# The first chunk's normalization on ScalarE and VectorE, its turns a block ahead, and two loads moved, in an attention and GLU kernel on one Trainium2 core

## The chip, the cores and the metric

The kernel runs on one core of a Trainium2 chip. The time is device microseconds of one execution. Six runs of the kernel before are shown by their median; one more execution was profiled.

The engines are written as the profile writes them: PE is TensorE (matmuls; PEld its weight loads), DVE is VectorE, ACT is ScalarE, POOL is GpSimd, and SP is SyncE, which here issues DMAs. SPq and ACTq are the queues through which SP and ACT issue DMAs.

## The reference

x has 2048 tokens of 512 values, all in bf16. One normalization of x feeds both parts.

```python
xn = (x - mean(x)) / sqrt(var(x) + 1e-5)

# A: attention, 32 heads of 16, each token sees the 256 tokens up to itself
q, k, v = split(xn @ wqkv)                      # wqkv 512 x 1536
p = softmax(where(0 <= i - j < 256, q @ k.T / 4, -1e9))
a = (p @ v) @ wo                                # wo 512 x 512

# B: gated bilinear, F = 1792
b = ((xn @ w_gate) * (xn @ w_up)) @ w_down

out = x + a + b
```

## The kernel before

The 2048 tokens are worked in four chunks T = 0..3 of 512 tokens, each of four blocks b of 128 tokens. For each chunk there are 14 gate groups `gT.f` and 14 up groups `uT.f` (four matmuls of 128x512 each, a "dense group"), projections to queries, keys and values, scores and weighted values of the attention, and the sums `downT.b` of 14 matmuls with `Wd` and four with `Wo`, which end in one PSUM bank and are added to x and stored. The sums of the last chunk are cut into two `Sums`: `down3.b` and `wo3.b`.

The program order is made when the kernel is built. The class `Kernel` holds a planner: `list_work` lists the work, and `loop` (line 309) plays it through with costs and due times written in the code (for example `PSUM_COPY`, and `land`, `wv`, `wk`, `wq` in `first_chunk`), emitting instructions in the order it arrives at. On the chip each engine runs its instructions in that order and waits for semaphores. What the planner knows are:

- `Op`: a step on DVE (`V`), ACT (`A`), POOL (`G`) or SP (`S`), with the engines that may take it and their costs. Copies out of PSUM may go to DVE or ACT.
- the list `A` of `Dense` groups for PE, of which the planner looks at the first `WINDOW` = 4, and the list `B` of `Sums`, of which only the first is looked at.
- scores: 76 batches S0 to S75, each eight to twenty small matmuls into one PSUM tile `S`, then an exponential on ACT (`P<-S`, line 476) of up to 2048 columns; no batch can start before the exponential of the one before has read `S`. `PACE` = 3.0 is the least distance between batches in the plan. Parts of P are then masked, either by selects on POOL (`i_select`, line 209) or by ANDs on DVE (`i_and`, line 215).
- values: V0 to V15, one after the batches of a (chunk, head group) pair, followed on DVE by two transposes, a reciprocal, a product and a transpose back.

Four PSUM banks `M0` to `M3` hold what PE writes for all but the scores; a bank is free again when a copy on DVE or ACT has read it.

`prologue` issues the loads. `x` of block 0, then `Wqkv` in three parts (values at 1024, keys at 512, queries at 0), then gate and up weights in halves, the rest of `x`, `Wd` and `Wo` go through SP's queue; `x` of blocks 1 to 3 goes through ACT's. POOL makes the identity matrix `ident`, and PE then runs 40 warm-up matmuls on it (line 180). ACT runs one exponential on a single column (line 170), which brings its function table in.

`first_chunk` is about chunk 0, the part most changed. Per block: `i_stats` (lines 241 to 243: statistics, mean and variance `mv`, and `ve` = variance + 1e-5) on DVE, `i_root` (line 247: `rs` = `ve` to the power -0.5) on POOL, `i_apply` (line 252: `xn` = (x - mean) * rs) on DVE, `turn` (line 576: four transposes of `xn` on PE), a copy to `xnT`, and then on PE the values `v0.b` (line 634), keys `k0b{b}` and queries `q0b{b}` (16 matmuls of 128x128 each). They are added to the list `A` block by block:

```python
self.add(f"turn{b}", 1.1, [ap], turn, turned)
self.add_v(0, b, wv)
self.add(f"k0b{b}", 4.2, [("xnT", 0, b), wk], lambda i, f=project: f(i, 512), k_out)
self.add(f"q0b{b}", 4.2, [("xnT", 0, b), wq], lambda i, f=project: f(i, 0), q_out)
```

With the window of four, PE's order comes out as turn0, v0, k0, turn1, q0, turn2, k1, q1, k2, q2, turn3, v1, v2, v3, k3, q3, g0.0, u0.0, S0 (v0 for `v0.0`, k0 for `k0b0` and so on). Blocks of later chunks are normalized by `norms` in the shadow of other work and transposed by DMA.

Of the kernel before, what the change touches and what calls it, by code (L numbers as in the profile page):

```python
# [8 lines left out]
F32 = mybir.dt.float32  # L9
# [76 lines left out]
class Kernel:  # L86
    PBUFS = 7
    WINDOW = 4
    PACE = 3.0
    SHARE = 1.0  # L90

    def __init__(self, live=True):
        self.live = live
# [4 lines left out]
    def open(self, ctx, tc, x, wqkv, wo, wg, wu, wd, out):  # L98
        self.tc, self.nc = tc, tc.nc
        self.x_d, self.out_d = x.flatten_outer_dims(), out.flatten_outer_dims()  # L100
        self.w_d = dict(qkv=wqkv, o=wo, g=wg, u=wu, d=wd)
        self.F = wg.shape[1]

        def pool(name, bufs, **kw):
            return ctx.enter_context(tc.tile_pool(name=name, bufs=bufs, **kw))

        c = self.const = pool("const", 1)
        self.work, self.few = pool("work", 3), pool("few", 2)
        psum = pool("psum", 1, space=bass.MemoryType.PSUM)

        def some(name, n, shape, dtype=BF16):
            return [c.tile(shape, dtype, name=f"{name}{i}") for i in range(n)]

        self.x = c.tile([128, NT, 512], BF16, name="x")
        self.Wqkv = c.tile([128, 4, 1536], BF16, name="Wqkv")
        self.Wo = c.tile([128, 4, 512], BF16, name="Wo")
        self.Wg = c.tile([128, 4, self.F], BF16, name="Wg")
        self.Wu = c.tile([128, 4, self.F], BF16, name="Wu")
        self.Wd = c.tile([128, NF, 512], BF16, name="Wd")
        self.Q = some("Q", 2, [128, 4, 512])  # L120
        self.K = some("K", 3, [128, 4, 8, 2, 64])
        self.V = some("V", 3, [128, 8, 16, 18])
        self.xnT = some("xnT", 2, [128, 4, 512])
        self.hT = some("hT", 2, [128, NF, 512])
        self.OT = some("OT", 2, [128, 4, 512])
        self.P = some("P", self.PBUFS, [128, 4, 512])
        self.xn = some("xn", 4, [128, 512])
        self.mv = some("mv", 2, [128, 4, 2], F32)
        self.rs = some("rs", 2, [128, 4], F32)
        self.ve = c.tile([128, NT], F32, name="ve")  # L130
        self.at = c.tile([128, 16, 2, 32], F32, name="at")
        self.on = c.tile([128, 16, 2, 16], BF16, name="on")
        self.ident = c.tile([128, 128], BF16, name="ident")
        self.own = c.tile([128, 2], F32, name="own")
        self.mhalf = c.tile([128, 4], F32, name="mhalf")
        self.masks = c.tile([128, 5, 64], I16, name="masks")
        self.S = psum.tile([128, 4, 512], F32, name="S")
        self.M = [psum.tile([128, 512], F32, name=f"M{i}") for i in range(4)] + [self.S[:, 3, :]]

    def prologue(self):  # L140
# [4 lines left out]
        def load(eng, dst, src):  # L145
            eng.dma_start(out=dst, in_=src)

        load(nc.sync, self.x[:, 0, :], xv[:, 0, :])
        for t in range(1, 4):
            load(nc.scalar, self.x[:, t, :], xv[:, t, :])  # L150
        for lo in (1024, 512, 0):
            load(nc.sync, self.Wqkv[:, :, lo:lo + 512], w["qkv"][:, :, lo:lo + 512])
        h = self.F // 2
        for lo in (0, h):
            load(nc.sync, self.Wg[:, :, lo:lo + h], w["g"][:, :, lo:lo + h])
# [1 line left out]
            if lo == 0:  # L157
                load(nc.sync, self.x[:, 4:8, :], xv[:, 4:8, :])
        load(nc.sync, self.x[:, 8:NT, :], xv[:, 8:NT, :])
        load(nc.sync, self.Wd[:], w["d"])  # L160
        load(nc.sync, self.Wo[:], w["o"])

        c = self.const
# [3 lines left out]
        nc.gpsimd.memset(self.mhalf[:], -0.5)  # L167
        warm = c.tile([128, 1], F32, name="warm")
        nc.vector.memset(warm[:], 0.0)
        nc.scalar.activation(out=warm[:], in_=warm[:], func=ACT.Exp)  # L170
        pi = c.tile([128, 1], I32, name="pi")
        nc.gpsimd.iota(pi[:], pattern=[[0, 1]], base=0, channel_multiplier=1)
        podd = c.tile([128, 1], I32, name="podd")
# [166 lines left out]
    def choose(self):  # L340
# [25 lines left out]
        for n, d in enumerate(self.A[:self.WINDOW]):  # L366
            t = self.when(d.deps)
            if t is not None and free:
                t = max(t, free[0][0], now)
                t += SWITCH * (d.mode != self.mode) + SWITCH * (d.mode == "C" and self.mode == "D")  # L370
                if a is None or t < a[0]:
                    a = (t, n)
        if self.B:
            d = self.B[0]
            t = self.when(d.deps)
            if t is not None and ("bank" in d.link or free):
                b = max(t, now if "bank" in d.link else max(now, free[0][0]))
# [148 lines left out]
    def list_work(self):  # L526
        self.first_chunk()
        for T in range(NCH):
            if T + 1 < NCH:
                self.norms(T + 1)  # L530
            for f in range(NF):
                self.add_gate(T, f)
            if T + 1 < NCH:
                self.add_qk(T + 1, 0)
                for b in range(4):
                    self.add_v(T + 1, b)
                for c in range(1, 4):
                    self.add_qk(T + 1, c)
        for T in range(NCH):
            for b in range(4):  # L540
                self.add_down(T, b)

    def add(self, *a):
        self.A.append(Dense(*a))
# [6 lines left out]

    def first_chunk(self):

        land = (3.7, 3.7, 4.6, 5.2)
        wv, wk, wq = 6.3, 7.8, 9.3
        st = [self.op(f"st{b}", {"V": (0.96, 1.05)}, [land[b]], lambda e, b=b: self.i_stats(b, self.mv[0]), rank=3 + b)
              for b in range(4)]
        roots = []
        for lo, hi in ((0, 1), (1, 2), (2, 4)):
            r = self.op(f"rs{lo}", {"G": (0.6 if hi - lo == 1 else 0.73, 0.62 if hi - lo == 1 else 0.75)}, st[lo:hi],  # L560
                        lambda e, lo=lo, hi=hi: self.i_root(0, lo, hi - lo), rank=0)
            roots += [r] * (hi - lo)
        last = self.op("masks", {"G": (0.33, 0.4)}, [r], lambda e: self.nc.gpsimd.memset(self.masks[:], -1), rank=9)
        for n in range(5):
            last = self.op("masks", {"G": (0.4, 0.5)}, [last], lambda e, n=n: self.i_masks(n), rank=9)
        self.at_["masks",] = last
# [2 lines left out]
                self.V[n][:, :, :, 16:18], 1.0), rank=9)  # L569
        for b in range(4):  # L570
            tok = slice(128 * b, 128 * b + 128)
            ap = self.op(f"ap{b}", {"V": (0.38, 0.48)}, [roots[b]], lambda e, b=b: self.i_apply(b), rank=0)

            def turn(i, b=b):
                for k in range(4):
# [26 lines left out]
                for c in range(4):  # L602
                    self.at_["Q", 0, c, b] = x

            self.add(f"turn{b}", 1.1, [ap], turn, turned)
            self.add_v(0, b, wv)
            self.add(f"k0b{b}", 4.2, [("xnT", 0, b), wk], lambda i, f=project: f(i, 512), k_out)
            self.add(f"q0b{b}", 4.2, [("xnT", 0, b), wq], lambda i, f=project: f(i, 0), q_out)
# [85 lines left out]
    def add_down(self, T, b):  # L694
        h = [("up", T, f) for f in range(NF)]
        o = [("OT", T, c) for c in range(4)]
        if T < NCH - 1:
            emit, evac = self.sum_of(T, b, slice(0, 512))
            self.B.append(Sums(f"down{T}.{b}", T, b, 0, 18, h + o, 2, emit, evac, {}))
            return  # L700
        late = [] if b < 2 else [("attended", T)]
        halves = [(slice(0, 512), {}, MM)]
        if b == 3:
            halves = [(slice(0, 256), {}, MM / 2), (slice(256, 512), {"bank": 4}, MM / 2)]
            late += [("S", len(self.batches) - 1)]
        for n, (cols, link, mm) in enumerate(halves):
            emit, evac = self.sum_of(T, b, cols)
            name = f"{T}.{b}{'ab'[n]}"
            self.B.insert(len(self.B) - b - n, Sums("down" + name, T, b, 0, NF, h + late, 7, emit, lambda o, i: None, link, mm))
            self.B.append(Sums("wo" + name, T, b, NF, 18, o, 4, emit, evac, link, mm))  # L710

    def sum_of(self, T, b, cols):
        tok, t, keep = slice(128 * b, 128 * b + 128), 4 * T + b, {}
# [60 lines left out]
```

## Time and profile before

| | |
|---|---|
| median of six runs | 269.22 us (268.84 to 269.45) |
| profiled execution | 268.92 us |
| its span | 266.9 us |
| PE busy | 260.7 us, 98% |
| DVE busy | 189.5 us, 71% |
| ACT busy | 163.6 us, 61% |
| POOL busy | 123.0 us, 46% |
| DMA in the second of 40 slices (6.67 us each) | 376 GB/s |

How to read the profile: a timeline line gives the start in us from the span's start, the time it took, engine, line of the kernel, operation, what it writes and reads, shapes, and the count of instructions merged into it; in square brackets stands how long the engine was idle before it and what released it. A line of waits gives who waited, for whom, the total in us, how often, and the longest. The chain of work that ended last is followed back from the last instruction, at each step to what released it; its lines give start, duration and what it was. PE's matmuls are pipelined and the shown durations overlap, so the distances between starts tell more than the durations.

### The profile page before, as it was taken

How to read it: one execution, taken by the hardware profiler on the slowest of the kernel's cores; microseconds unless marked ns; L12 is line 12 of the kernel's file. 1: busy time of each engine (PE TensorE's matmuls, PEld its weight loads, DVE VectorE, ACT ScalarE, POOL GpSimd, SP SyncE). 2: the span in 40 equal slices, each digit the busy share in tenths (PEclk: the TensorE clock that was granted, in tenths of full speed). 3: DMA queues.
4: the chain of work that ended last, by engine and by line, in shares of the span. 5: the costliest groups of instructions: out<-in, count | busy, mean ns of one | idle time of the engine just before them, and what ended most of it. 6: DMA issues, size and time to landing. Idle time of an engine off the chain costs nothing.

```text
span 266.9 us, 7983 instructions
## 1 busy us (share of the span) xinstructions
PE 260.7 (98%) x3450; PEld 131.1 (49%) x3450; DVE 189.5 (71%) x361; ACT 163.6 (61%) x118; POOL 123.0 (46%) x276
## 2 busy tenths in 40 slices
PE   7999999999999999999999999999999999999994
PEld 6884344654544444464443444356443444353562
DVE  5879978879995717788997716878882628778224
ACT  2315666877786566768677567667786567657100
POOL 3501675646357180735539180825537180825500
PEclk9999999999999999999999999999999999999999
DMA  6999630000003010000002210000000000000002
GB/s 229 376 375 348 172 42 2 4 0 2 4 13 69 22 41 25 0 2 2 0 2 48 57 39 22 0 4 2 2 2 20 22 23 22 0 2 0 2 2 79
DMA packets 17186, 13.87 MB, mean 52 GB/s; under 512 B 7040, under 2 KB 17152, under 8 KB 17152
## 3 DMA queue, kind: packets, MB, share of 16 engines
q1 hardware_dynamic: 16576, 12.91, 15.9%
q8 instruction: 27, 0.44, 0.7%
q10 hardware_dynamic: 576, 0.46, 0.5%
q14 instruction: 7, 0.06, 0.1%
HBM read 9.70 MB, written 2.10 MB: 44 GB/s over the span
## 4 chain that ended last, share of the span: by engine, by line
PE 95%; DVE 1%; DMA 1%; ACT 1%; issue 0%
PE M L192 72%; PE S L200 9%; PE M L224 7%; PE M L634 6%; DMA x<-in_A_x_dram 1%; ACT P L476 1%; PE S L192 1%; DVE st L241 0%; PE M L576 0%; DVE xn L724 0%; ACT xnT L186 0%; DVE mv L242 0%; DVE xn L252 0%; DVE ve L243 0%
## 5 line engine op out<-in xcount | busy, mean ns | idle before, releaser
L476 ACT ACTIVATE P<-S 128x2048 bf16<-128x2048 f32 x76 | 140.9, 1853 | 57.0 <-PE S L200 54.3
L209 POOL TENSOR_SCALAR_AFFINE_SELECT P<-P 64x256 bf16<-64x256 bf16 (+1 forms) x248 | 113.7, 460 | 116.9 <-ACT P L476 104.0
L192 PE MATMUL M<-xnT,Wg 128*128 128x512 bf16 x224 | 57.7, 380 | 0.0
L192 PE MATMUL M<-xnT,Wu 128*128 128x512 bf16 x224 | 57.7, 380 | 0.0
L192 PE MATMUL M<-Wd,hT 128*128 128x512 bf16 (+1 forms) x224 | 51.5, 373 | 0.0
L685 DVE TENSOR_TENSOR hT<-M,gsb 128x512 bf16<-128x512 f32 x56 | 38.0, 679 | 9.2 <-PE M L192 8.9
L192 PEld LDWEIGHTS <-hT 128*128 128x128 bf16 x238 | 21.6, 98 | 24.2 <-issue 3.2
L192 PEld LDWEIGHTS <-Wu 128*128 128x128 bf16 x224 | 20.4, 98 | 25.3 <-issue 2.8
L512 DVE STREAM_TRANSPOSE at<-M 128x512 f32<-128x512 f32 x32 | 22.3, 707 | 14.6 <-PE M L224 14.6
L192 PEld LDWEIGHTS <-Wg 128*128 128x128 bf16 x224 | 19.9, 98 | 24.9 <-issue 4.1
L192 PE MATMUL M<-xnT,Wqkv 128*128 128x128 bf16 (+1 forms) x224 | 30.6, 288 | 0.0
L200 PE MATMUL S<-Q,K 32*128 32x320 bf16 (+3 forms) x720 | 30.0, 254 | 0.1
L188 DVE CAST gsb<-M 128x512 bf16<-128x512 f32 x36 | 24.7, 686 | 5.4 <-PE M L192 5.2
L200 PEld LDWEIGHTS <-K 32*128 32x128 bf16 x720 | 12.0, 92 | 32.1 <-issue 31.1
L215 DVE TENSOR_TENSOR P<-P,masks 128x512 int16<-128x512 int16 x56 | 23.0, 418 | 6.2 <-ACT P L476 6.2
L724 DVE TENSOR_TENSOR y<-M,x 128x512 bf16<-128x512 f32 x12 | 8.3, 688 | 20.5 <-PE M L192 20.3
L263 DVE TENSOR_SCALAR K<-M,own 128x512 bf16<-128x512 f32 x27 | 19.2, 745 | 4.6 <-PE M L192 4.6
L192 PEld LDWEIGHTS <-Wqkv 128*128 128x128 bf16 x224 | 15.7, 98 | 11.0 <-issue 1.8
L224 PE MATMUL M<-P,V 64*17 64x320 bf16 (+4 forms) x1440 | 21.0, 252 | 0.0
L224 PEld LDWEIGHTS <-V 64*17 64x17 bf16 x1440 | 16.6, 85 | 2.6 <-issue 0.8
L186 ACT ACTIVATE gsb<-M 128x512 bf16<-128x512 f32 x20 | 12.0, 598 | 9.6 <-PE M L192 7.3
L634 PE MATMUL M<-Wqkv,xnT 128*64 128x256 bf16 x256 | 15.7, 274 | 0.7 <-ACT xnT L186 0.7
(44 smaller groups left out, 140.9 us busy)
## 6 DMA issues: line engine op xcount, KB each, us to landing
Wg<-in_B_w_gate_dram SPq DMA_DIRECT2D x2, 896.0 KB, 10.7
Wu<-in_B_w_up_dram SPq DMA_DIRECT2D x2, 896.0 KB, 12.2
Wd<-in_B_w_down_dram SPq DMA_DIRECT2D x1, 1792.0 KB, 17.3
Wqkv<-in_A_wqkv_dram SPq DMA_DIRECT2D x3, 512.0 KB, 6.2
out_dram<-y SPq DMA_DIRECT2D x12, 128.0 KB, 1.7
x<-in_A_x_dram SPq DMA_DIRECT2D x1, 1024.0 KB, 15.2
x<-in_A_x_dram SPq DMA_DIRECT2D x1, 512.0 KB, 12.1
Wo<-in_A_wo_dram SPq DMA_DIRECT2D x1, 512.0 KB, 13.2
```

The lines of the kernel that those rows point to most:

```text
L186: self.nc.scalar.activation(out=out, in_=in_, func=ACT.Copy)
L188: self.nc.vector.tensor_copy(out=out, in_=in_)
L192: self.nc.tensor.matmul(ps, lhsT=a, rhs=b, start=first and n == 0, stop=last and n == len(pairs) - 1)
L200: self.nc.tensor.matmul(self.S[:, e, 64 * at:64 * (at + m)], lhsT=self.K[U % 3][rows, c, j].rearrange("p l t -> p (l t)"), rhs=self.Q[T % ...
L209: self.nc.gpsimd.affine_select(out=v, in_=v, pattern=[[0, 4], [0, n], [sign, 64]], base=0, fill=0.0, compare_op=ALU.is_gt if kind else ALU ...
L215: self.nc.vector.tensor_tensor(out=v, in0=v, in1=m, op=ALU.bitwise_and)
L224: self.nc.tensor.matmul(banks[lane][32 * e:32 * e + 17, 64 * q:64 * (q + m)], lhsT=self.V[U % 3][rows, j, 4 * c + e, 0:17], rhs=P[rows, e, ...
L263: self.nc.vector.tensor_scalar(out=out, in0=in_, scalar1=own, scalar2=None, op0=ALU.mult)
L476: ex = self.op(f"exp{g}", {"A": (took + 0.06, took + 0.18)}, [o], lambda e: self.nc.scalar.activation(out=P[:, :, 0:hi], in_=self.S[:, :, ...
L512: t = self.op(f"tr{v}", {"V": (0.63, 0.71)}, [o] + ts, lambda e, par=par: nc.vector.transpose(out=self.at[:, :, par, :], in_=self.M[banks[ ...
L634: self.nc.tensor.matmul(self.M[i][64 * lane:64 * lane + 64, 256 * jj:256 * jj + 256], lhsT=self.xnT[T % 2][:, k, tok], rhs=w[:, lane], sta ...
L685: x = self.op(f"u{T}.{f}", {"V": PSUM_COPY["V"]}, [o, ("gate", T, f)], lambda e: self.nc.vector.tensor_tensor(out=self.hT[T % 2][:, f, :], ...
```

## The change

- `first_chunk`: each block's inverse deviation is made by a square root on ACT with 1e-5 as its bias, and a reciprocal on DVE. `i_root` on POOL is used by `norms` alone now. The statistics of block 1 stand behind the normalizing of block 0 in the plan (`FIRST`).
- ACT's first table is that of the square root; a one-column exponential, planned behind the four roots, brings in the table of the exponential ("table").
- `turn1` to `turn3` are put two places before the end of the list, that is, before the keys and queries of the block before.
- x of block 2 is loaded behind the key weights and x of block 3 behind the query weights, both through SP's queue. `Wd` is loaded in five parts.
- The mask steps on POOL are due at 6.0 instead of behind the last root. The costs and due times in `first_chunk` are others, and `PACE` is 2.95.
- The sums of the last chunk: `down3.b` is cut into two halves of seven matmuls that need only their own up groups, and the order is by block; the planner looks at them only once the list `A` is empty.

With these, the order on PE at the start is turn0, v0, turn1, k0, q0, k1, turn2, q1, v1, v2, k2, turn3, q2, k3, q3, g0.0, u0.0, S0, v3. At the end, before: S74, g3.13, u3.13, S75, three pieces of seven matmuls of the last sums, V15, the other pieces. After: S73, g3.9, u3.9, g3.10, S74, u3.10, g3.11, u3.11, S75, g3.12, u3.12, g3.13, u3.13, one piece of seven, V15, the other pieces. In between the same groups come in a slightly shifted order.

```diff
-    PACE = 3.0
+    PACE = 2.95
     SHARE = 1.0
+    FIRST = True
...
+        self.eps = c.tile([128, 1], F32, name="eps")
...
         load(nc.sync, self.x[:, 0, :], xv[:, 0, :])
-        for t in range(1, 4):
-            load(nc.scalar, self.x[:, t, :], xv[:, t, :])
-        for lo in (1024, 512, 0):
+        load(nc.scalar, self.x[:, 1, :], xv[:, 1, :])
+        for n, lo in enumerate((1024, 512, 0)):
             load(nc.sync, self.Wqkv[:, :, lo:lo + 512], w["qkv"][:, :, lo:lo + 512])
+            if n:
+                load(nc.sync, self.x[:, n + 1, :], xv[:, n + 1, :])
...
-        load(nc.sync, self.Wd[:], w["d"])
+        for f, g in ((0, 3), (3, 6), (6, 9), (9, 12), (12, 14)):
+            load(nc.sync, self.Wd[:, f:g], w["d"][:, f:g])
         load(nc.sync, self.Wo[:], w["o"])
...
-        nc.scalar.activation(out=warm[:], in_=warm[:], func=ACT.Exp)
+        nc.vector.memset(self.eps[:], 1e-5)
+        nc.scalar.activation(out=warm[:], in_=warm[:], func=ACT.Sqrt)
+        self.warm = warm
...
-        if self.B:
+        if self.B and (self.B[0].T < NCH - 1 or not self.A):
...
+        self.last = []
         for T in range(NCH):
             for b in range(4):
                 self.add_down(T, b)
+        self.B += [d for _, d in sorted(self.last, key=lambda x: x[0])]
...
-        land = (3.7, 3.7, 4.6, 5.2)
-        wv, wk, wq = 6.3, 7.8, 9.3
-        st = [self.op(f"st{b}", {"V": (0.96, 1.05)}, [land[b]], lambda e, b=b: self.i_stats(b, self.mv[0]), rank=3 + b)
-              for b in range(4)]
-        roots = []
-        for lo, hi in ((0, 1), (1, 2), (2, 4)):
-            r = self.op(f"rs{lo}", {"G": (0.6 if hi - lo == 1 else 0.73, 0.62 if hi - lo == 1 else 0.75)}, st[lo:hi],
-                        lambda e, lo=lo, hi=hi: self.i_root(0, lo, hi - lo), rank=0)
-            roots += [r] * (hi - lo)
-        last = self.op("masks", {"G": (0.33, 0.4)}, [r], lambda e: self.nc.gpsimd.memset(self.masks[:], -1), rank=9)
+        land = (3.75, 3.9, 7.9, 9.6)
+        wv, wk, wq = 6.1, 7.3, 9.1
+        nc = self.nc
+        applied, roots = [], []
+        for b in range(4):
+            keep = {}
+
+            def bn(e, b=b, keep=keep):
+                keep["st"] = self.work.tile([128, 6], F32, tag="st", name="st")
+                nc.vector.bn_stats(out=keep["st"][:], in_=self.x[:, b, :])
+                nc.vector.bn_aggr(out=self.mv[0][:, b, :], in_=keep["st"][:])
+
+            s = self.op(f"st{b}", {"V": (0.92, 0.94)}, [land[b]] + applied * (b == 1 and self.FIRST), bn, rank=3 + b)
+            s = self.op(f"sq{b}", {"A": (0.20, 0.25)}, [s], lambda e, b=b: nc.scalar.activation(
+                out=self.ve[:, b:b + 1], in_=self.mv[0][:, b, 1:2], func=ACT.Sqrt, bias=self.eps[:]), rank=0)
+            roots.append(s)
+            s = self.op(f"rs{b}", {"V": (0.15, 0.16)}, [s], lambda e, b=b: nc.vector.reciprocal(
+                out=self.rs[0][:, b:b + 1], in_=self.ve[:, b:b + 1]), rank=0)
+            applied = [self.op(f"ap{b}", {"V": (0.38, 0.48)}, [s], lambda e, b=b: self.i_apply(b), rank=0)]
+            self.at_["ap", b] = applied[0]
+        self.op("table", {"A": (1.5, 1.5)}, roots, lambda e: nc.scalar.activation(
+            out=self.warm[:], in_=self.warm[:], func=ACT.Exp), rank=1)
+        last = self.op("masks", {"G": (0.33, 0.4)}, [6.0], lambda e: self.nc.gpsimd.memset(self.masks[:], -1), rank=9)
...
-            ap = self.op(f"ap{b}", {"V": (0.38, 0.48)}, [roots[b]], lambda e, b=b: self.i_apply(b), rank=0)
+            ap = self.at_["ap", b]
...
-            self.add(f"turn{b}", 1.1, [ap], turn, turned)
+            at = len(self.A) - 2 if b else 0
+            self.A.insert(at, Dense(f"turn{b}", 1.1, [ap], turn, turned))
...
-            self.B.insert(len(self.B) - b - n, Sums("down" + name, T, b, 0, NF, h + late, 7, emit, lambda o, i: None, link, mm))
-            self.B.append(Sums("wo" + name, T, b, NF, 18, o, 4, emit, evac, link, mm))
+            for m, lo in enumerate((0, 7)):
+                hi = lo + 7
+                self.last.append(((0, b, n, m), Sums(
+                    "down" + name, T, b, lo, hi, h[:hi] + late, 7, emit, lambda o, i: None, link, mm)))
+            self.last.append(((2, b, n), Sums("wo" + name, T, b, NF, 18, o, 4, emit, evac, link, mm)))
```

## The prediction

> **What bounds the kernel.** I read the page first. TensorE (PE) is busy 98% of the span, and the chain that ended last is 95% PE. So a change counts only where PE waits, where it does fewer things, or where the work starts sooner.
>
> ```profile
> PE 260.7 (98%) x3450; PEld 131.1 (49%) x3450; DVE 189.5 (71%) x361; ACT 163.6 (61%) x118; POOL 123.0 (46%) x276
> ...
> PE 95%; DVE 1%; DMA 1%; ACT 1%; issue 0%
> ```
>
> Next, the waits of PE alone. There are three and the first is the warm-up, so PE has almost nothing to wait for between 7.2 and 263 us:
>
> ```profile
> PE M L180 <- POOL mhalf L167: 1.4, 1, 1.4
> PE M L634 <- ACT xnT L186: 0.7, 1, 0.7
> PE M L576 <- DVE xn L252: 0.2, 1, 0.2
> ```
>
> Third, the timeline of the first 14 us. It shows how block 0 comes to PE: statistics, the addition on VectorE (DVE), the power on GpSimd (POOL), normalizing, four transposes, copy, first product.
>
> ```profile
> 1.43 4.45 PE L180 MATMUL M<-ident 128*128 128x128 bf16 x40 [1.43 <-POOL mhalf L167]
> ...
> 2.19 1.28 ACT L170 ACT_TABLE_LOAD   x1 [2.19 <-issue]
> 3.48 0.20 ACT L170 ACTIVATE warm<-warm 128x1 f32<-128x1 f32 x1
> 3.58 0.69 DVE L241 BATCH_NORM_STATS2 st<-x 128x6 f32<-128x512 bf16 x1 [1.64 <-DMA x<-in_A_x_dram]
> 4.31 0.18 DVE L242 BATCH_NORM_AGGREGATE mv<-st 128x2 f32<-128x6 f32 x1
> 4.53 0.15 DVE L243 TENSOR_SCALAR ve<-mv 128x1 f32<-128x1 f32 x1
> ...
> 4.84 0.56 POOL L247 TENSOR_TENSOR rs<-ve,mhalf 128x1 f32<-128x1 f32 x1 [3.07 <-DVE ve L243]
> ...
> 5.60 0.41 DVE L252 TENSOR_SCALAR xn<-x,mv,rs 128x512 bf16<-128x512 bf16 x1
> ...
> 6.07 0.42 PE L576 MATMUL M<-ident,xn 128*128 128x128 bf16 x4 [0.19 <-DVE xn L252]
> 6.53 0.60 ACT L186 ACTIVATE xnT<-M 128x512 bf16<-128x512 bf16 x1 [2.84 <-PE M L576]
> ...
> 9.45 0.90 PEld L192 LDWEIGHTS <-Wqkv 128*128 128x128 bf16 x16 [0.16 <-DMA Wqkv<-in_A_wqkv_dram]
> ```
>
> Last, the chain in order of time near the end: 1.89 us in which PE's next scores stand behind the exponential of the last, as only two dense groups (four matmuls each) lie between these two batches.
>
> ```profile
> 243.36 0.36 PE S L200 x8
> ...
> 243.74 1.89 ACT P L476
> ...
> 245.67 0.40 PE S L200 x8
> 246.07 4.64 PE M L192 x21
> ```
>
> **The start.** Removed: four additions (0.15 each) and three powers (0.56, 0.66, 0.70). Added per block: a square root on ScalarE (ACT) and a reciprocal on DVE. Neither is in the trace. The square root of 128x1 lies between 0.20 (the warm-up ACTIVATE) and 0.29 (0.20 plus the 0.09 by which the key copies with a pointer scale, 687 ns, exceed the plain copies, 598); I take 0.25. The reciprocal lies between 0.15 (one-column DVE rows) and 0.34 (128x32, L508); I take 0.15, the row with its width. For DVE to ACT I take 0.05, for ACT to DVE 0.03 (146.14 to 146.17 us); the DVE-POOL crossings of 0.16 and 0.20 bound them above.
>
> Block 0: variance at 4.49; root 4.54 to 4.79; reciprocal 4.82 to 4.97; normalizing 5.00 to 5.41; PE could begin at 5.46 instead of 6.07. But the 40 warm-up matmuls stand before it on PE: by the start times in the trace they come 0.107 apart and the last starts at 5.565, so the turn starts at 5.67. All unknowns at their upper ends (root +0.04, reciprocal +0.19, crossings +0.3) would make it 5.99, still below 6.07. A gain on the warm-ups is impossible, as their matmuls and their start (POOL's identity) are untouched. The turn is slower there: the four matmuls of the first turn started 0.080, 0.067, 0.056 apart, later ones 0.056, so PE came to full rate at about 6.16 us. At 0.107 each the last starts at 5.99 and, with the 0.255 that the first one took, ends at 6.25; copy 6.29 to 6.89; values of block 0 at 6.93 against 7.17. **Gain 0.24** (at full rate the turn would end 0.19 sooner, 0.43; next to nothing at the unknowns' upper ends).
>
> [...]
>
> **The turns a block ahead.** Program order is now turn0, v0, turn1, k0, q0, k1, turn2, q1, v1, v2, k2, turn3, q2, k3, q3. With the rows' lengths (v 1.00, a projection 0.90, a turn 0.22) turn1 stands at 7.93. Its block: the second statistics 5.42 to 6.33 (behind the first normalizing), the root waits on ACT behind the 0.60 copy until 6.91, reciprocal 7.19 to 7.34, normalizing to 7.78, PE from 7.83. It fits, with 0.10 to spare.
>
> **The loads.** x of blocks 2 and 3 leaves ACT's queue (its issue falls from 1.36 to about 0.45 us, so the table load at 2.19 comes sooner, which nothing needs) for SP's, behind the key and query weights: two issues of 0.4 us, which every later SP load waits for, and 256 KB that no longer run beside the first weights. Before, the query weights held PE from 9.29 to 9.45. Only 128 KB (x of block 3) now goes behind them: at the 375 GB/s of the page's second slice 0.35 us, landing at about 9.1. PE asks at 7.93+0.22+0.90 = 9.05, so q0 starts at 9.1, 0.35 before its old 9.45: the 0.24 above and **gain 0.11** here. Were they no sooner than 9.45, both would be lost; with no wait at all it is 0.16. x of block 2 has 1.41 MB up to its end. The trace's packets started 1.25 MB by 6.0 and 1.62 MB by 7.0 us, and the query weights ended 1.1 us after their last packet: landing near 7.6. Its statistics stand at 7.78 on DVE; turn2 has 0.35 more. x of block 3, near 9.4, is wanted at 11.3. Gate and up weights start 0.8 us later on SP and are wanted at 17.8 and 18.6, where their first halves' packets ended at 10.7 and 13.1. The down weights in five loads add four issues; SP had its last load out at 24.02 and is wanted at 29.26, the weights near 85: nothing.
>
> **The second table load.** ACT now loads the exponential's table (1.28, then 0.20) behind the fourth root. That root follows the statistics of block 3 (DVE 11.29 to 12.20), so ACT is taken from 12.25 to 13.94. Behind it stand a value copy (PE hands it over at 14.0) and the copy of turn3 (15.3): no cost. [...]
>
> **The order after it.** Values of block 3 move behind the first scores: same work. Masks are due earlier on POOL and are first used at 30.8: nothing. The pace of 2.95 per batch of 76 pulls the scores forward. In the program order S73, S74 and S75 now have three dense groups (2.70) between them and four behind S75. At the old place the last matmul before S75 started at 245.14 and S75 at 245.67, 0.53, where the other 74 places show 0.31. **Gain 0.21.** The last V (weighted values) stands 0.33+2.70+0.33+2.70+0.33+4.96+0.22 = 11.6 after S73; POOL's last 16 selects began 2.58 after S73 and took 7.71, 10.3: 1.3 to spare. 42 matmuls of 0.216 (9 us) lie behind V, and its normalizing took 3.2, so the output products do not wait. Unbroken stretches on PE number 178, not 179; each costs about 0.11 (twelve matmuls 2.70, sixteen 3.56). **Gain 0.11.**
>
> **Sum:** 0.24+0.11+0.21+0.11 = 0.67. The profiled execution took 268.92 (span 266.9 and 2.0 around it), 0.30 under the median of 269.22; so 268.25 for such an execution, **268.55** as a median.
>
> **Rivals.** [...] *The front stands still*: turn1's spare of 0.10 and turn3's (normalized at 14.76, PE at 14.84) are eaten by the unknowns, and the 0.24 and 0.11 go; 0.32 is left: 268.9. For it: three engine crossings now in place of two. *Slower:* the quicker pace puts ten matmuls (2.16+0.11+0.33 = 2.60) between two batches in seven places, two before; a batch waits for the last exponential, and the spare before at such a place was 0.21 (exponential over at 143.54, next scores 143.74). Each place with a 0.60 copy ahead of its exponential loses 0.39; it ends slower from four places on; at all seven, 2.7: 271.2. Against it: the order on ACT has no copy between those exponentials.
>
> **How the numbers follow.** About 0.2% (0.54 us) is what a measurement can tell from no change. Forecast 0.65; switch 0.17; front 0.10; slower 0.08. Of the forecast some five sixths pass 0.54, of the front a little: faster 0.56. Same: the switch, most of the front and the rest of the forecast, 0.35. Slower 0.09. The range runs from 268.1 (the turn at full rate and q0 without a wait are worth 0.24 more, and the six runs lie up to 0.4 from their median, of which 0.2 is taken) to 269.2 (the switch); the slow case is left out.
>
> **What would show it.** First turn at 5.67, values of block 0 at 6.93, q0 at 9.1, the first dense group at 17.8 instead of 19.0 (0.9 of it the moved values), S75 0.31 behind the matmul before it. Wrong if ACT's load row is followed by more than 0.1 of idle, if PE's waits name DVE or ACT after 10 us, or if scores in mid-span start later than 0.31 after the last dense matmul.

## The result, and the profile after

The changed kernel takes 267.98 us (median of 33 runs, 267.46 to 269.26) where the kernel before takes 269.21 (68 runs, 268.82 to 270.63): a ratio of 0.9956, 95% interval 0.9946 to 0.9965. It is faster by 1.2 us; 0.67 was forecast, and 267.98 lies below the range of 268.1 to 269.2.

Eleven of the 68 runs before and nine of the 33 after lie some 1.35 us above the rest, so a median "of the lower group" below leaves those out: 269.11 before (57 runs), 267.82 after (24), a gain of 1.29. The profiled execution of after (269.26) is one of the upper group. A second execution of the same kernel, e1 below (267.86), is not, and is compared with the profiled execution of before (268.92).

Two lines tell the groups apart. The first is from the timeline of after, the second from that of e1: the sixteen matmuls of the first values, which start at the same time.

```profile
7.06 1.92 PE L656 MATMUL M<-Wqkv,xnT 128*64 128x256 bf16 x16 [0.69 <-ACT xnT L192]
```

```profile
7.06 1.06 PE L656 MATMUL M<-Wqkv,xnT 128*64 128x256 bf16 x16 [0.69 <-ACT xnT L192]
```

In after they still run at the slow rate (1.92). The trace's first record of the granted clock (1.0) begins at 10.80 us in after, at 6.67 in e1 and at 6.16 in before, and behind it the distances of the matmuls are about half (in after, those of 128x128 fall from 0.107 to about 0.06 us).

The busy times and the shares of the chain, from the page of e1:

```profile
PE 260.5 (98%) x3450; PEld 131.1 (49%) x3450; DVE 193.3 (73%) x369; ACT 162.5 (61%) x117; POOL 120.0 (45%) x273
...
PE 94%; DMA 3%; SPq 1%; DVE 1%; issue 0%
```

PE is as busy as before (260.7). New in the chain is DMA with 3%: it runs through the query weights, issued at 2.83 us and landed 6.66 later. The waits of PE in e1:

```profile
PE M L186 <- POOL ident L169: 1.4, 1, 1.4
PE M L656 <- ACT xnT L192: 0.7, 1, 0.7
PE M L198 <- DMA Wqkv<-in_A_wqkv_dram: 0.2, 1, 0.2
```

The warm-up and the first copy are as before; the wait for the normalizing (0.2) is below what this view lists, the one for the query weights is there. Neither DVE nor ACT is named after 10 us. The start of e1 in the timeline:

```profile
3.40 0.69 DVE L571 BATCH_NORM_STATS2 st<-x 128x6 f32<-128x512 bf16 x1 [1.46 <-DMA x<-in_A_x_dram]
4.13 0.18 DVE L572 BATCH_NORM_AGGREGATE mv<-st 128x2 f32<-128x6 f32 x1
...
4.35 0.29 ACT L575 ACTIVATE ve<-mv,eps 128x1 f32<-128x1 f32 x1 [1.62 <-DVE mv L572]
4.67 0.16 DVE L578 RECIPROCAL rs<-ve 128x1 f32<-128x1 f32 x1 [0.36 <-ACT ve L575]
4.88 0.83 DVE L258 TENSOR_SCALAR xn<-x,mv,rs 128x512 bf16<-128x512 bf16 x1
4.98 0.59 POOL L589 MEMSET V<- 128x256 bf16 x2
...
5.77 0.61 PE L597 MATMUL M<-ident,xn 128*128 128x128 bf16 x4
...
7.42 0.41 DVE L258 TENSOR_SCALAR xn<-x,mv,rs 128x512 bf16<-128x512 bf16 x1
...
9.54 1.96 PE L198 MATMUL M<-xnT,Wqkv 128*128 128x128 bf16 x32 [0.19 <-DMA Wqkv<-in_A_wqkv_dram]
...
12.12 0.28 ACT L575 ACTIVATE ve<-mv,eps 128x1 f32<-128x1 f32 x1
...
12.42 1.28 ACT L582 ACT_TABLE_LOAD   x1
...
13.72 0.20 ACT L582 ACTIVATE warm<-warm 128x1 f32<-128x1 f32 x1
...
14.52 0.60 ACT L192 ACTIVATE V<-M 128x512 bf16<-128x512 f32 x1 [0.60 <-PE M L656]
```

The root takes 0.29, the upper end of what was forecast (0.25 was taken), and the reciprocal 0.16 (0.15). The first normalizing takes 0.83, beside POOL's memsets of the ones of V; the next takes 0.41. The second table load stands between its neighbours with 0.02 on either side, and ACT is idle 0.60 before its next copy. Near the end, the chain of e1 in order of time:

```profile
235.93 0.33 PE S L206 x8
236.26 2.69 PE M L198 x12
238.96 0.33 PE S L206 x8
239.29 2.69 PE M L198 x12
241.98 0.33 PE S L206 x8
242.31 5.07 PE M L198 x23
```

The last three batches have 2.7 us of dense work between them, and no exponential is in the chain any more.

**Where the time went.** Each profiled execution is cut at two starts on PE: the first dense group, and its last matmul.

| us | before | e1 (after) | less by |
|---|---|---|---|
| start: to the first dense group | 19.01 | 18.22 | 0.79 |
| middle: to PE's last matmul | 243.85 | 244.34 | -0.49 |
| ending: to the end of the span | 4.02 | 3.59 | 0.43 |
| outside the span | 2.04 | 1.71 | 0.33 |
| sum | 268.92 | 267.86 | 1.06 |

The sixteen value matmuls of block 3 moved from the start to the middle; by the distances of those matmuls they are 0.87. So in these two executions the start lost 0.08, the middle gained 0.38, and **0.76 of 1.06 lies behind the start of PE's last matmul**, where the forecast had nothing. The operations there are the same in both: four products, the additions, the stores. The view by windows, from the end of DVE's last addition to the span's end (start:end, length, busy time by engine, clock, DMA share, GB/s), first of before, then of e1:

```profile
263.66:266.88 3.22, 0.00 (x0) 0.00 (x0) 0.00 (x1) 0.00 (x0) 0.00 (x0) 0.80 0.26 81
```

```profile
263.36:266.15 2.79, 0.00 (x0) 0.00 (x0) 0.00 (x1) 0.00 (x0) 0.00 (x0) 0.99 0.31 97
```

No engine computes in it: the last stores land, and then the engines close by waits on semaphores and drains, which the trace records one by one.

### The profile page after: what moved, and what is told of

It is laid out like the page before. It is cut to its first block, busy times and chain, and to the rows that moved or that the text cites. A ratio compares the mean times of both kernels' runs of the same rounds, so it can differ in the third digit from the quotient of the medians.

```text
span 267.5 us, 7984 instructions
## 1 busy us (share of the span) xinstructions
PE 262.1 (98%) x3450; PEld 132.5 (50%) x3450; DVE 193.1 (72%) x369; ACT 162.5 (61%) x117; POOL 120.0 (45%) x273
## 4 chain that ended last, share of the span: by engine, by line
PE 97%; DMA 1%; DVE 1%; ACT 0%; POOL 0%; issue 0%; POOLq 0%
PE M L198 71%; PE S L206 9%; PE M L230 7%; PE M L656 6%; PE M L186 2%; DMA out_dram<-xn 1%; PE S L198 1%; PE M L597 1%; DVE xn L749 1%; ACT xnT L192 0%; POOL ident L169 0%; POOL ident L168 0%; POOLq L169 0%; POOLq L783 0%
## 5 line engine op out<-in xcount | busy, mean ns | idle before, releaser
L194 DVE CAST gsb<-M 128x512 bf16<-128x512 f32 x43 | 29.4, 684 | 5.8 <-PE M L198 5.7
L198 PE MATMUL M<-xnT,Wqkv 128*128 128x128 bf16 (+1 forms) x224 | 31.5, 294 | 0.0
L269 DVE TENSOR_SCALAR K<-M,own 128x512 bf16<-128x512 f32 x28 | 20.1, 742 | 4.7 <-PE M L198 4.4
L198 PEld LDWEIGHTS <-Wqkv 128*128 128x128 bf16 x224 | 16.6, 101 | 11.0 <-issue 1.9
L656 PE MATMUL M<-Wqkv,xnT 128*64 128x256 bf16 x256 | 16.5, 283 | 0.7 <-ACT xnT L192 0.7
L198 PE MATMUL M<-Wo,OT 128*128 128x512 bf16 (+1 forms) x64 | 15.7, 373 | 0.0
```

Of the source, the lines that this page charges most:

```text
L194: self.nc.vector.tensor_copy(out=out, in_=in_)
L198: self.nc.tensor.matmul(ps, lhsT=a, rhs=b, start=first and n == 0, stop=last and n == len(pairs) - 1)
L269: self.nc.vector.tensor_scalar(out=out, in0=in_, scalar1=own, scalar2=None, op0=ALU.mult)
L656: self.nc.tensor.matmul(self.M[i][64 * lane:64 * lane + 64, 256 * jj:256 * jj + 256], lhsT=self.xnT[T % 2][:, k, tok], rhs=w[:, lane], sta ...
```

## The experiments

Theories at the outset: PE comes to its full rate at an instant that differs from run to run, and the gain beyond the forecast is in the new start (C); the start gives the forecast 0.35, and the rest comes from the order of the last work (O). After e1 to e4 came a third: four more loads of `Wd` shorten the closing waits of SP (E). After e5 to e8 came a fourth: an engine halts for 0.35 to 0.5 us at a fixed place of its instruction stream, and how many records (instructions of that engine in the trace) precede the ending decides whether that place falls where it is seen (F).

**e1**, the changed kernel again. No edit.

> The changed kernel once more, for a second profile and more times. Its first profile (269.26 us) shows PE at half rate until 10.8 us (first values of block 0 0.207 apart from 7.06 to 8.55), before's shows full rate from 6.16. Theory C (clock): PE's rate changes at an instant that differs from run to run; where it comes early the first turn starts below 5.67, since the 40 warm-ups end sooner, and the first dense group (Wg) starts at about 17.2 to 17.5 (17.8 was forecast, 19.01 in before); where it comes late, at about 19.6 as in the first profile. Theory O (order): the front gains the forecast 0.35 at the same rate of PE (dense group at 17.8), and what is more lies behind it. Both: times in two clusters, near 267.8 and 269.2.

267.74 (before 269.28; ratio 0.9946, 0.9934 to 0.9958), all five runs in the lower group. Its profile is shown above: the first dense group starts at 18.22, where C expected 17.2 to 17.5 for an early full rate and O 17.8.

**e2**, the new start alone (with the five loads of `Wd`): `PACE` 3.0 and the last sums as before.

```diff
-    PACE = 2.95
+    PACE = 3.0
-        if self.B and (self.B[0].T < NCH - 1 or not self.A):
+        if self.B:
...
+            self.B.insert(len(self.B) - b - n, Sums("down" + name, T, b, 0, NF, h + late, ...))
+            self.B.append(Sums("wo" + name, T, b, NF, 18, o, 4, emit, evac, link, mm))
```

> Only the front of the change (roots, turns, loads, tables), with the pace of 3.0 and the last sums as before. The change as a whole gave 1.2 us. Theory C: the front is the larger part, 0.7 to 0.9 us faster than before. Theory O: the forecast 0.35 faster, no more. The front stands still: 0 to 0.1.

**e3**, the rest alone: the kernel before with `PACE` 2.95 and the new last sums.

```diff
-    PACE = 3.0
+    PACE = 2.95
-        if self.B:
+        if self.B and (self.B[0].T < NCH - 1 or not self.A):
...
+        self.B += [d for _, d in sorted(self.last, key=lambda x: x[0])]
```

> Only the pace of 2.95 and the new last sums, with the old front; three unbroken PE stretches fewer than before (176 for 179, at 0.11 each) and S75 without its 0.21. Theory C: 0.4 to 0.55 us faster than before. Theory O: 0.8 to 1.0 faster, as the front gives only 0.35.

e2: 268.32, ratio 0.9967 (0.9955 to 0.9979). e3: 268.63, ratio 0.9978 (0.9961 to 0.9995). The new start gives the larger part, and as much as C expected (0.7 to 0.9). But in the profiled executions most of it is not on PE: PE's last matmul starts only 0.25 sooner in e2 (262.61 against 262.86), ending and outside are 0.15 and 0.27 shorter. In e3 the middle is 0.57 shorter, ending and outside nearly as before (3.97, 1.97), and the median less far down than O expected (0.8 to 1.0).

**e4**, six matmuls on the identity behind the first turn (`fill`), into the bank of the scores.

```diff
+                for _ in range(6 if b == 0 else 0):
+                    self.nc.tensor.matmul(self.S[:, 0, 0:128], lhsT=self.ident[:], rhs=self.ident[:], start=True, stop=True)
```

> The changed kernel with six more 128x128 matmuls on the identity (result unused, into the scores' bank) behind turn0, so that PE does not idle from 6.1 to 7.05 us while ACT copies. If the late rate comes from that gap (theory C), the slow cluster near 269.2 goes or gets rare (it was 9 of 33), and the fast one stays near 267.8. If the late rate has nothing to do with the gap, a quarter of the times stay near 269.2. If the six delay the first values, the fast cluster is 0.1 to 0.3 later.

267.77, ratio 0.9947 (0.9935 to 0.9959): as e1, and none of its five runs is in the upper group. The first normalizing began sooner here (4.75), took 0.41, and the first turn began at 5.665.

**e5** and **e6**, theory E: the kernel before with `Wd` in five loads, and the changed kernel with `Wd` in one.

```diff
-        load(nc.sync, self.Wd[:], w["d"])
+        for f, g in ((0, 3), (3, 6), (6, 9), (9, 12), (12, 14)):
+            load(nc.sync, self.Wd[:, f:g], w["d"][:, f:g])
```

> The kernel before with one edit: the down weights in five loads instead of one. PE waits for none of them. So far PE's last matmul starts only 0.30 us sooner in the second profile of the changed kernel (262.56) than in before's (262.86), while the time from it to the end of the span fell from 4.02 to 3.59 and what lies outside the span from 2.04 to 1.71. Theory E (end): the four more DMAs shift which of the eight DMA semaphores the last stores use, SP's closing waits then come in the order of landing, and the end gets shorter without any gain on PE: 3.5 to 3.75 from PE's last matmul to the end, 0.3 to 0.7 us faster in all. Theory P (PE): the end differs for another reason and this edit is worth 0.0 to 0.1.

> The changed kernel with the down weights in one load, as in before. Theory E: the end is long again, 3.9 to 4.05 from PE's last matmul to the end of the span, and the time 0.3 to 0.7 us above the changed kernel's (268.1 to 268.5 where that has 267.8). Theory P: the time of the changed kernel, within 0.1.

e5: 269.58, ratio 0.9997 (0.998 to 1.0014), ending 4.00: no gain. e6: 267.79, ratio 0.9931 (0.9907 to 0.9955), no loss in time, though its ending is 3.86, 0.27 longer than in e1. E falls as stated. That the longer ending of e6 does not show in its median of six runs is open, for theory F too.

**e7**, the ones of V on DVE, later, so that nothing runs beside the first normalizing.

```diff
-            last = self.op("ones", {"G": (0.26, 0.33)}, [last], lambda e, n=n: self.nc.gpsimd.memset(
+            self.op("ones", {"V": (0.15, 0.2)}, [25.0 + 4 * n], lambda e, n=n: self.nc.vector.memset(
```

> The changed kernel with the two memsets of ones into V1 and V2 on DVE, planned at 29 and 33 us, instead of on POOL behind the masks. In the changed kernel they ran on POOL from 4.98 to 5.56, and the first normalizing on DVE beside them took 0.73 and 0.83 instead of 0.41. If the two share something: that normalizing takes 0.41, the first turn starts at 5.67 behind the last warm-up instead of 5.77, and the front gains 0.1. If not, the first normalizing stays near 0.75 and nothing changes.

267.97, ratio 0.9946 (0.9927 to 0.9965). In its timeline

```profile
4.85 0.41 DVE L258 TENSOR_SCALAR xn<-x,mv,rs 128x512 bf16<-128x512 bf16 x1
...
5.67 0.41 PE L597 MATMUL M<-ident,xn 128*128 128x128 bf16 x4
```

the normalizing takes 0.41 and the first turn starts at 5.67, the forecast's bound by the warm-ups. The median did not gain by it: 2.11 us lie outside the span here, 0.40 more than in e1.

**e8**, the changed kernel with the roots made the old way, by addition and power, and nothing else put back.

```diff
+                nc.vector.tensor_scalar(out=self.ve[:, b:b + 1], in0=self.mv[0][:, b, 1:2], scalar1=1e-5, scalar2=None,
+                                        op0=ALU.add)
-            s = self.op(f"sq{b}", {"A": (0.20, 0.25)}, [s], lambda e, b=b: nc.scalar.activation(
-                out=self.ve[:, b:b + 1], in_=self.mv[0][:, b, 1:2], func=ACT.Sqrt, bias=self.eps[:]), rank=0)
+            s = self.op(f"sq{b}", {"A": (0.20, 0.25)}, [s], lambda e, b=b: self.i_root(0, b, 1), rank=0)
```

> The changed kernel with the old way to the inverse deviations: addition of 1e-5 on DVE and power on POOL per block, everything else, order and table loads too, as in the changed kernel. By the rows of before (addition 0.15, power 0.56 to 0.66, crossings 0.16 and 0.20) block 0 is normalized by 5.9 and turn0 starts at about 5.97 instead of 5.77, and turn1, whose power waits behind mask selects on POOL too, at about 8.5 instead of 8.05: 0.2 to 0.6 us slower than the changed kernel if roots are what the front gains by; within 0.1 of it if the query weights' landing (9.1 to 9.5) is what the front ends on.

267.46, ratio 0.9926 (0.99 to 0.9953): not slower, against what was expected. Its timeline:

```profile
4.27 0.15 DVE L573 TENSOR_SCALAR ve<-mv 128x1 f32<-128x1 f32 x1
4.58 0.56 POOL L253 TENSOR_TENSOR rs<-ve,mhalf 128x1 f32<-128x1 f32 x1 [2.81 <-DVE ve L573]
...
5.09 0.36 POOL L584 MEMSET masks<- 128x320 int16 x1
5.17 0.42 DVE L258 TENSOR_SCALAR xn<-x,mv,rs 128x512 bf16<-128x512 bf16 x1 [0.75 <-POOL rs L253]
...
5.67 0.63 PE L597 MATMUL M<-ident,xn 128*128 128x128 bf16 x4
```

From the end of the variance to the start of the normalizing the old way takes 0.94 (4.23 to 5.17), the new one 0.57 (4.31 to 4.88); but the old one holds POOL, so that the ones start only at 10.13 and not beside the first normalizing, which takes 0.42 and ends at 5.59 where the new one ends at 5.71. But the powers also bring POOL to 333 records, and e8's ending is 3.29 against 3.59 in e1 (theory F below), so its median is better compared with e9 and e16, whose endings are 3.31 and 3.27: 267.46 against 267.56 and 267.6, on other chips, with a first dense group at 18.10 against 17.70 and 17.92. The exchange of the engines bought nothing that these runs show. What the start gains would then come from its order and loads, which no run here took apart.

**e9** to **e12**, theory F: eight one-column memsets more on POOL in the changed kernel (behind the ones), and on POOL, DVE or ACT of the kernel before (in the prologue; ACT by copies of one column).

```diff
+        for n in range(8):
+            last = self.op("pad", {"G": (0.05, 0.1)}, [last], lambda e: self.nc.gpsimd.memset(pad[:], 0.0), rank=9)
```

> The changed kernel with eight more one-column memsets on POOL behind the masks and ones, where nothing waits for POOL. [...] Theory N: the end depends on other things (work of the last microseconds, spread between runs): 3.59 and 267.8.

> The kernel before with eight more one-column memsets on POOL at the start (329 records become 337), beside warm-ups, done before its first power. Theory F: its closing gap on POOL (2.997 to 3.372 behind PE's last matmul) goes: 3.6 to 3.75 to the end of the span instead of 4.02, 0.3 us faster. Theory N: 4.0, no change.

> The kernel before with eight more one-column memsets on DVE at the start (439 records become 447; the changed kernel has 446), done before the first x lands. [...]

> The kernel before with eight more one-column copies on ACT at the start (221 records become 229; the changed kernel has 213), done by 5.4 us, before its first copy at 6.5. [...]

e9: 267.56, ratio 0.993 (0.9909 to 0.9952): with eight instructions more the median is 0.2 below e1's, on another chip and with intervals that overlap. The same window as above is, in e9,

```profile
262.84:265.34 2.50, 0.00 (x0) 0.00 (x0) 0.00 (x1) 0.00 (x0) 0.00 (x0) 1.00 0.35 108
```

0.29 shorter than in e1, and POOL's halt of 0.37 (from 3.03 to 3.40 us behind the start of PE's last matmul) is gone, as theory F has it. e10: 269.18, ratio 0.9996 (0.9981 to 1.0011): POOL's halt is gone there too, but SP's remains (3.04 to 3.52), the ending is 3.86, and the gain of 0.3 that was expected did not come. e11: 269.08, ratio 0.999 (0.9975 to 1.0004), outside the span 1.83 instead of 2.04, too little to be clear in the median. e12: 269.17, ratio 0.9987 (0.9975 to 0.9999), 2.04, no effect of ACT in the ending.

**e13** and **e14**, the halts together: the kernel before with `Wd` in five loads and the eight memsets on POOL; and with eight on DVE as well.

> The kernel before with Wd loaded in five parts and eight one-column memsets more on GpSimd, so that both SP (85 records in place of 81) and GpSimd (336 in place of 329) have moved past the places in their instruction streams at which each halted for 0.4 to 0.5 us behind PE's last matmul. Each of the two alone gave 0.1 us at most, as the other halt stayed. [...] Rival 'the ending belongs to the order of the last sums': 3.9 to 4.0, and a median within 0.15 of the kernel before.

> The same with eight one-column memsets more on VectorE too (447 records). Theory: the time outside the span, 2.04 us before and 1.71 after, holds a halt of VectorE's or another engine's stream; with VectorE's moved it is 1.75 to 1.85 and the median 0.15 to 0.25 below that of the kernel with the two other edits. Rival 'another engine sets it': 2.0 to 2.05, no difference.

e13: 269.1, ratio 0.9993 (0.9974 to 1.0011), which holds five runs of the upper group; the lower group is 268.88 against 269.22, 0.34 sooner. The ending is 3.57, just outside the 3.3 to 3.5 expected by theory F, and the gain short of the 0.45 expected, for SP still halts from 2.20 to 2.67. e14: 268.59, ratio 0.9975 (0.9957 to 0.9993); lower group 268.53, 0.35 below e13, and outside the span 1.83 instead of 2.04, as the theory has it. Its start is that of the kernel before: the first dense group is at 19.29.

**e17** and **e18**, SP's count alone. e17 is e14 with `Wd` in six loads, one record more on SP; e18 is the fastest form of the changed kernel (e16 below) with `Wd` in four, one record less.

> The kernel before with eight one-column memsets more on GpSimd and on VectorE and Wd loaded in six parts in place of one, so that SP has 86 records, one more than with five parts. With five parts SP still halted from 2.20 to 2.67 us behind the start of PE's last matmul, past the landing of the last store at about 2.45. Theory 'a halt at a fixed place of each stream': with one record more the halt falls earlier, under the wait for the last store, the stretch behind PE's last matmul takes 3.27 to 3.32 us in place of 3.55, and the median of most runs is 268.2 to 268.4 (0.25 below the same with five parts). Rival 'SP's halt has to do with the loads themselves, not with their number': 3.5 to 3.6, no difference from five parts.

> The reverse: the changed kernel with the six fillers and the eight memsets on GpSimd (267.6), and Wd loaded in four parts in place of five, so that SP has 85 records in place of 86. Theory: SP's halt moves to 2.20 to 2.67 us behind the start of PE's last matmul, the stretch to the span's end takes 3.53 to 3.57 us in place of 3.27, and the median is 267.75 to 267.9, 0.25 slower for one transfer less. Rival: 3.25 to 3.35 and 267.5 to 267.6.

e17: 268.4, ratio 0.9966 (0.9952 to 0.9979); lower group 268.25, ending 3.33, outside 1.85. Its window is as short as that of e9:

```profile
265.19:267.72 2.53, 0.00 (x0) 0.00 (x0) 0.00 (x1) 0.00 (x0) 0.00 (x0) 0.81 0.35 107
```

e18: 267.78, ratio 0.9948 (0.9935 to 0.996), ending 3.78 (3.53 to 3.57 was expected) against 3.27 in e16: one load less makes the ending half a us longer, and the median 0.18 above that of e16 (on another chip). SP's halts, read from the gaps between its closing records:

| records on SP | kernels | SP's halt, us behind the start of PE's last matmul |
|---|---|---|
| 81 | before, e10 | 3.04 to 3.52 |
| 82 | e6 | 2.86 to 3.33 |
| 85 | e2, e5, e13, e14 | 2.20 to 2.68 |
| 85 | e18 | 2.42 to 2.90 |
| 86 | after, e1, e9 | 1.89 to 2.37 |

The more records, the earlier the halt; with 86 it lies under the wait for the last store, which lands at about 2.45, and the ending is 3.33 in e17, against 3.55 in e14 with 85. POOL's goes the same way: 3.00 to 3.37 with 329 records (its drain), 3.03 to 3.40 with 326, 3.39 to 3.76 with 325, none with 333 or more.

The place can be counted in the traces. On SP the halt stands between the 79th and the 80th record in all 19 profiled executions with 81 records or more (0.47 to 0.49 us from start to start, 0.74 in e17); e3 has 79 records, and no halt. On POOL it stands between the 324th and the 325th in all eleven with 325 to 329 records; e7 has 324, and none in the span. With 333 or more that place falls 15 to 18 us before PE's last matmul, and no halt is seen there (0.07 between the two records in e8 and e9). One engine without its halt is not enough: the ending is 3.97 in e3, where POOL's stays, and 3.86 in e10, where SP's stays, against 3.55 to 3.57 in e13 and e14.

**F holds**: in e17 only the numbers of instructions in three streams were changed (memsets that nothing reads, one transfer cut in six), and it is 0.98 faster than the kernel before by the lower groups.

**e15** and **e16**: the kernel before with the six fillers of e4; and the changed kernel with them and with eight memsets on POOL between the masks and the ones.

> The kernel before with six matmuls on the identity behind the first turn, into the scores' bank, which is still unused: they fill the 1.0 us in which PE waits for the first copy (6.3 to 7.1 us). The median of most runs stays at 269.1 to 269.3. [...]

> The changed kernel with the six matmuls on the identity behind the first turn, and eight one-column memsets on GpSimd between the masks and the ones of V, so that no memset of ones runs beside the first normalizing and GpSimd's halt behind PE's last matmul is gone. Expected: first normalizing 0.41 us, first turn at 5.67, first dense group at 17.9 to 18.0, from PE's last matmul to the end 3.3, median 267.3 to 267.5, none of the runs near 269. If the pads bring only what the ending shows: 267.5; if neither holds, 267.8 as the changed kernel.

e15: 269.3, ratio 0.9995 (0.9981 to 1.0008), the twelve runs within 269.04 to 269.46. e16: 267.6 (267.23 to 267.96), ratio 0.9931 (0.9914 to 0.9948). In e16's timeline

```profile
4.97 1.36 POOL L590 MEMSET pad<- 128x1 f32 x8
5.10 0.41 DVE L258 TENSOR_SCALAR xn<-x,mv,rs 128x512 bf16<-128x512 bf16 x1
...
5.67 0.51 PE L600 MATMUL M<-ident,xn 128*128 128x128 bf16 x4
```

the normalizing stands beside one-column memsets and takes 0.41. First dense group at 17.92, ending 3.27: as expected; the median is at 267.6, 0.1 above the expectation. e9 and e8 are as fast within their intervals, and the lower groups of all three are 0.2 to 0.4 below that of the changed kernel, on other chips.

On one chip, with e13 to e16, 15 of the 53 runs without the fillers lie in the upper group and none of the 18 with them; e4 and e18 add ten without one. All four profiled executions of the upper group (after, e5, e13, e17) came to the full rate at 10.7 to 10.8 us, the others at 4.3 to 7.1 where that can be read. So the upper group is a late full rate, and PE's pause of 1 us behind the first turn has a part in it; why the rate is late in some executions only, no record here shows.

## Why the prediction was right or wrong

The direction was right, the amount was not: a gain of 1.29 by the lower groups, 0.67 in the sum. In the two executions that were compared, the four terms of the sum gave 0.30 together, and 0.76 came from a stretch that the sum had left as it was.

**The step that failed is none of the four terms but what was left out.** The sum was taken from "span 266.9 and 2.0 around it", and both the 2.0 and the stretch behind PE's last matmul were carried over unchanged, without a reason; of the four more loads of `Wd` the prediction said: "nothing". The 2.0 shrank by 0.33 and that stretch by 0.43. The change does not touch the work there; with its two loads of x on SP's queue and four further loads of `Wd`, SP has five records more in all (81 to 86), which moves SP's halt under the last store. It also moves POOL from 329 to 326 and DVE from 439 to 446. No view of the profile of before showed this; the records of the closing sequence did, a gap of 0.5 on SP and of 0.4 on POOL. That the part of DVE lies outside the span rests on three runs (1.83 to 1.85 with 447 records, 2.04 with 439 in the same kernel), but e2 has 437 and 1.77, so DVE's count alone does not decide it: the other engines of that 0.33 stay open. The 2.11 of e7, with 324 records on POOL, would be POOL's halt gone beyond the span; that is argued, not shown.

With the endings made alike the forecast comes near: e17 (268.25) against e9 (267.56) is 0.69, of which 0.14 is still outside the span (1.85 and 1.71), so some 0.55 for start and middle together, where 0.67 was forecast. This rests on five runs each, on two chips.

**First turn, 0.24.** The bound by the warm-ups at 5.67 is right (e4, e7, e8, e16), and root, reciprocal and crossings are within the bounds given. Missed was POOL: "masks are due earlier on POOL ... nothing". The masks pull the ones forward with them, to 4.98, onto the first normalizing, which takes 0.64 to 0.86 instead of 0.41 (after, e1, e2, e6, e9); in e1 the turn starts at 5.77 and the values of block 0 at 7.06, where 5.67 and 6.93 were forecast. With the ones moved away it takes 0.41 in e7 (0.83 beside them in e1), but in e8 the memset of the masks stood beside the normalizing and left it at 0.42, so which memsets do it, and by what, is open.

The prediction took the full rate to begin at 6.16, as in the one profile of before. "A gain on the warm-ups is impossible" held only for executions whose full rate begins behind them: in e3 it began at 4.34, and the warm-ups were over at 5.0; in e18 at 5.38, and the turn started at 5.54.

**Query weights, 0.11.** They held PE until 9.54 in e1 instead of the forecast 9.1, so the two terms of the start gave -0.08 between these two executions, where 0.35 was forecast. The landing is loose: queries start at 9.29 to 10.05 in seven executions with the old start, at 9.02 to 9.54 in nine with the new. Before's profiled execution (9.45) was an early one and e1's a late one, which one profile each couldn't tell. Over executions at full rate, the first dense group is at 19.37 on average with the old start (seven, 19.01 to 19.60) and at 17.99 with the new (nine, 17.70 to 18.22). That would be a gain of 0.51; these kernels carry pads and other edits, so it is a hint that the new start is worth at least the 0.35 that was forecast, no measurement.

**The ending's order on PE, 0.21 and 0.11.** Right: S75 stands 0.31 behind the matmul before it, and the middle gained 0.38 in e1 and 0.57 in e3, in place of 0.32. There is one unbroken dense stretch fewer, as forecast; its 0.11 was not measured by itself. (Of the "other 74 places" in before, five behind value matmuls show 0.20, the rest 0.31; the term does not change by it.)

**The table load, nothing.** Right: 0.02 of idle on each side in e1, and a cover of 0.60 left. No run shows the loss at the switch to which the prediction gives 0.17 and the upper end of its range (269.2): the second load took 1.28 in e1, as the first one in before.

**The front stands still** and **slower by pace:** the spares of turn1 and turn3 held, and scores in mid-span start 0.31 behind the dense matmul before them, so neither came.

**The range** took in two uncertainties of the start and none of the ending. What would show it wrong, by the prediction's own list, did not occur. Of what would show it right, the first turn, the values, q0 and the first dense group came 0.10, 0.13, 0.44 and 0.42 later in e1 than said. The list had nothing on the ending.

## What to carry to other kernels

Cut a profiled execution at PE's last matmul before costing a small change, and ask of the stretch behind it, and of the time outside the span, what could move there: here, counts of instructions alone brought 0.98 (e17), where the whole change brought 1.29. A gain of half a microsecond from an edit is shown only when the same edit without its side effects (records, loads, what is pulled along on another engine) gives it too; here the exchange of the roots' engines gave nothing measurable, while sixteen memsets that nothing reads and one load cut in six made the kernel before 0.98 faster. Steps that are moved take along what is chained behind them: the ones followed the masks and met the normalizing.

## What the runs showed of the hardware

- SP halted once near the end in the 19 profiled executions with 81 records or more on it, mostly for 0.47 to 0.49 us (0.74 in e17) behind its 79th record, and POOL in the eleven with 325 to 329 records for 0.37 to 0.39 behind its 324th, so the halt came earlier the more records lay ahead of the ending. What an engine halts for, no record here shows.
- The clock's full rate began between 4.3 and 7.1 us in most executions and at 10.7 to 10.8 in others of the same kernel, worth some 1.35 us; with PE's pause of 1 us filled, no run of 28 lay in the upper group. What else sets the instant, no record here shows.
- One-column memsets beside the first normalizing left it at 0.41 us (e16), and the memset of the masks (128x320) at 0.42 (e8); beside the two memsets of the ones of V (128x256) it took 0.64 (e2) to 0.86 (e9).
